# The output projection of a fused attention and MLP kernel: from two slots a tile with partial sums in DRAM to four slots a tile without them

## The chip, the cores and the metric

One core of one Trainium2 chip runs the whole program. The metric is device time in microseconds (us) of one execution. The kernel before took 1678.53 us, the median of three runs (1677.63 to 1680.38).

## The reference, cut to what matters

```python
# x: [1, 2048, 512] f32; wqkv: [512, 1536]; wo: [512, 512]; w1: [512, 1792]; w2: [1792, 512]; H = 32, Dh = 16
xn = layernorm(x)
q, k, v = split(xn @ wqkv)                       # 32 heads of 16
s = softmax(q @ k.T * Dh**-0.5) @ v @ wo          # the last product is "WO" below
h = xn @ w1 + b1
r = where(h > 0, h, 0)
g = silu((r * r) @ w2 + b2)
out = x + s * g
```

## The kernel before, in words

**Units, slots, engines.** Attention is cut into 32 units (`NU`): a unit is four heads (a quad, eight of them) by 512 queries (a chunk, four of them), unit u being quad u // 4 and chunk u % 4. A unit has 16 slots, one for each 128 keys, so the main loop has 512 slots. In slot `st` TensorE makes four score products (`exp_mm`, tile `se`, line 1222), ScalarE takes their exponential (`pt`, line 1228), and the four value products of slot `st - 2` follow (`pv_step`, `pv_mm`, line 376; each is recorded as two matmuls, so eight records of line 376 are one slot). TensorE's order is written out by hand: it is the order in which the Python code emits.

**Maxima.** The exponential is shifted by a row maximum, from a second set of score products (`max_mm`, line 301, tile `pm_t`), 64 for each unit and 2048 in all, each reduced by VectorE (line 309). Unit u's maxima are due eight slots before its first slot (`SHIFT`). A few are made before the loop, and the rest in the slots, usually four in each. When a unit's maxima are complete, `shift` transposes them (line 337) two slots later and sends them by way of DRAM into the rows of `qe` that the scores read.

**Row tiles.** Scores and maxima contract over 64 rows: TensorE is split into two row tiles of 64 rows ("lanes"), and two such matmuls run side by side, one in each lane. Dense products (the MLP, and WO) contract over 128 rows and are cut into a lower and an upper half: one half runs in its lane while scores and maxima run in the other. Two lanes may not write one bank at once, so the halves of a product take turns. All f32 dense products are made from high and low parts: three matmuls for one product.

**Two ways to put dense work into slots.** `slot` (used for what `halves` yields) puts one half's products into one slot, opposite the scores and maxima of the other lane. `long_slots` (used for what `block` yields) takes 12 products of each half and lays them over four slots, a half over two slots. It knows two forms: where `ahead_m` says that the maxima are far enough ahead, a half gets seven maxima and the value products of its two slots stand together; else it gets eight maxima and the value products stand apart. The text calls them the form with seven and the form with eight.

**Order of the dense work.** The generator `dense` gives the loop its dense work: the MLP up to slot 451 (`mlp_tasks`, mostly `long_slots`), two slots with none, and then WO. Normalised attention rows come back from DRAM (`on_d`) as `oc`. `wo_part` makes, for 16 tiles of 128 tokens, the products with the first 384 rows of `wo` (quads 0 to 5; the last 128 rows belong to quads 6 and 7, which end late), two slots a tile by `halves`; for chunks 2 and 3 it adds quad 6's rows (`q6`, line 761). ScalarE copies the bank (line 751), GpSimd multiplies with the gate `g` and adds `x` (lines 752 and 753), and for chunks 0 and 1 the result goes to DRAM (`sp_d`). `wo_last` then adds the last 128 rows of `wo` for chunks 0 and 1, in 2 x 8 slots of three products a half; its result is multiplied by VectorE (line 781), added by GpSimd to the partial sum that is read back from `sp_d`, and stored. The last quad of chunks 2 and 3 is done by `unit_inner` and `unit_final` from the unit's own tile: three matmuls of 128 rows a tile (`unit_out`, line 828). `unit_final` is the chain behind the last value product: copy `po`, four sums (line 792), reciprocal, spreading (line 808), normalising, split into high and low, four `unit_out`, four stores.

**Banks.** PSUM has `pe` (3 banks, tile `se`), `pm` (3, tile `pm_t`), `pd` (1, tile `pd_t`, the dense products) and `pv` (1, tile `po`). After the last maximum `slot` and `plain_slot` lend every second score a `pm` bank. Before the loop, the last of the projection is drained by

```python
while far:
    step([lambda: max_mm(0)] + [None] * 4)
```

where `step` issues one entry of its list and one of `far` in turns.

Of the kernel before, what the change touches and what calls it, by code (L numbers as in the profile page):

```python
# [16 lines left out]
P = 128  # L17
# [23 lines left out]
def kernel(  # L41
# [21 lines left out]
    sp_d = dram.tile([S, D], F32, name="sp_d")  # L63
# [33 lines left out]
    with ExitStack() as ph:  # L97
# [558 lines left out]
        def wo_pools():  # L656
            wos["f"] = right(wstk, "fp", 4)
            wos["oc1"] = right(wstk, "oc1p", 1)
            tp = tail["p"] = right(wstk, "tailp", 1)
            wos["oc3"] = right(o3, "oc3p", 2)  # L660

        def wo_small():

            tp = tail["p"]
            raw = wos["f"].tile([P, D], F32, name="s")
# [12 lines left out]
        def wo_load(c, kos):  # L678
            if len(kos) > 1:
                oc = wos["oc3"].tile([P, 2, len(kos), 512], F32R, name="oc")  # L680
            else:
                oc = right(wstk, f"oc1{c}p", 1).tile([P, 2, 1, 512], F32R, name="oc") if c else wos["oc1"].tile([P, 2, 1, 512], F32R, name="oc")

            for a, b in ((0, P), (P, 512)) if len(kos) > 1 and c == 0 else ((0, 512),):
                for n, ko in enumerate(kos):
                    nc.sync.dma_start(
                        oc[:, :, n, a:b].bitcast(F32),
                        on_d[ko][:, :, c * 512 + a : c * 512 + b].rearrange("k p t -> p k t"),
                    )
            wos["t" if len(kos) > 1 else "l", c] = oc  # L690

        def wo_terms(ps, oc, tt, kos):
            wot = wos["w"]
            ts_ = slice(tt * P, (tt + 1) * P)
            return terms3(ps, [
                (lambda a, q, n=n: oc[q, a, n, ts_], lambda b, q, ko=ko: wot[q, b, ko])
                for n, ko in enumerate(kos)
            ])

        def wo_ask(k):  # L700

            c, tt = divmod(k % 16, 4)
# [3 lines left out]
            if k < 16:  # L706
                t = wos["oc3"].tile([P, D], F32, name="xr", bufs=3)
                nc.sync.dma_start(t, xf[t0 : t0 + P, :])
            elif c < 2:
                t = wos["f"].tile([P, D], F32, name="s")  # L710
                nc.sync.dma_start(t, sp_d[t0 : t0 + P, :])
            else:
                t = tail[c, tt]
            wos[k] = g, t

        def wo_part():
            q6s = []
            for c in range(4):
                for tt in range(4):
                    k = 4 * c + tt  # L720
                    if c < 3 and tt == (1 if c == 0 else 0):
                        wo_load(c + 1, [0, 1, 2])
                    if k in (4, 8):

                        q = wos["oc3"].tile([64, 2, 512], F32R, name="q6", bufs=2)
                        nc.sync.dma_start(
                            q.bitcast(F32),
                            on_d[3][:, :64, (k // 4 + 1) * 512 : (k // 4 + 2) * 512].rearrange(
                                "k p t -> p k t"
                            ),  # L730
                        )
                        q6s.append(q)
                    if k in (8, 12):
                        q6 = q6s.pop(0)
                    if k < 14:
                        wo_ask(k + 2)
                    if k == 14:
                        wo_load(0, [3])
                        wo_ask(16)
                        wo_ask(17)  # L740
                    ps = pd.tile([P, D], F32, name="pd_t")
                    t0 = c * 512 + tt * P
                    ts_ = slice(tt * P, (tt + 1) * P)
                    g, xr = wos.pop(k)
                    if c > 1:
                        s = tail[c, tt] = tail["p"].tile([P, D], F32, name=f"ts{c}{tt}")
                    else:
                        s = wos["f"].tile([P, D], F32, name="s")

                    def post():  # L750
                        nc.scalar.activation(s, ps, AF.Copy)
                        nc.gpsimd.tensor_tensor(s, s, g, op=ALU.mult)  # L752
                        nc.gpsimd.tensor_tensor(s, s, xr, op=ALU.add)  # L753
                        if c < 2:
                            later(2, lambda s=s, t0=t0: nc.sync.dma_start(sp_d[t0 : t0 + P, :], s))

                    it = halves(wo_terms(ps, wos["t", c], tt, [0, 1, 2]), (9,), post, 1)
                    own, end = next(it)
                    if c > 1:
                        own = own + [  # L760
                            lambda a=a, b=b: nc.tensor.matmul(
                                ps, q6[:, a, ts_], wos["w"][:64, b, 3],
                                start=False, stop=False, skip_group_check=True,
                            )
                            for a, b in ((0, 0), (0, 1), (1, 0))
                        ]
                    yield own, end
                    yield from it

        def wo_last(c):  # L770
            for tt in range(4):
                k = 16 + 4 * c + tt
                wo_ask(k + 2)
                if k == 19:
                    wo_load(1, [3])
                t0 = c * 512 + tt * P
                g, s = wos.pop(k)
                ps = pd.tile([P, D], F32, name="pd_t")

                def post():  # L780
                    nc.vector.tensor_tensor(g, ps, g, op=ALU.mult)
                    nc.gpsimd.tensor_tensor(g, g, s, op=ALU.add)
                    later(1, lambda g=g, t0=t0: nc.sync.dma_start(of[t0 : t0 + P, :], g))

                yield from halves(wo_terms(ps, wos["l", c], tt, [3]), (3,), post, 1)


# [36 lines left out]
        def unit_out(ps, c, tt, add):  # L824
            hl, w7 = tail["hl"], tail["w7"]
            ts_ = slice(tt * P, (tt + 1) * P)
            for n, (i, k) in enumerate(((0, 0), (0, 1), (1, 0))):
                nc.tensor.matmul(  # L828
                    ps, hl[:, i, ts_], w7[:, k], start=(n == 0), stop=(n == 2)
                )  # L830
            k = 16 + 4 * c + tt
            g, s = wos.pop(k)
            t0 = c * 512 + tt * P
            if k < 28:
                wo_ask(k + 2)
            if k == 27:
                later(2, lambda: [wo_ask(30), wo_ask(31)])
# [7 lines left out]
        def unit_inner(po):  # L845
# [7 lines left out]
            def out(tt):  # L853
                tail["hl"] = ev["hl"]
                unit_out(pm.tile([P, 512], F32, name="pm_t"), 2, tt, nc.gpsimd)
# [4 lines left out]
        def unit_final(po):  # L860
            ot = tail["ot"] = tail["p"].tile([P, 512], F32, name="tot")
            nc.scalar.activation(ot[:, :256], po[:, :256], AF.Copy)
# [3 lines left out]
            for tt in range(4):  # L866
                unit_out(
                    pm.tile([P, 512], F32, name="pm_t"), 3, tt, nc.vector if tt % 2 else nc.gpsimd
# [338 lines left out]
        while far:  # L1207
            step([lambda: max_mm(0)] + [None] * 4)
# [4 lines left out]

        def exp_mm(st, j, pts, spare):
# [3 lines left out]
            if spare:  # L1218
# [27 lines left out]
        def dense():  # L1246
# [4 lines left out]
            wo_load(0, [0, 1, 2])  # L1251
            wo_ask(0)
            wo_ask(1)
            for _ in range(2):
# [3 lines left out]
            for c in range(2):  # L1258
                if c == 0:
                    o3.close()  # L1260
                else:
                    for _ in range(4):
                        yield None, None
                yield from wo_last(c)
# [47 lines left out]
        def long_slots(st0, units, post):  # L1312
# [26 lines left out]
            for h in range(2):  # L1339
# [3 lines left out]
                if ahead_m(sum(done_m) + 7, st + 2):  # L1343
                    visit(h, "s" + "D" * 12 + "s", ".mmsmssmsmssmm")
# [5 lines left out]
                else:  # L1350
                    visit(h, "D" * 10, "msmsmsmsms")
# [4 lines left out]
                    visit(h, "DDss", "mmsm", True)  # L1356
# [36 lines left out]
        for st_ in range(NU * 16):  # L1393
# [11 lines left out]
            if item is not None and len(item) > 2:  # L1405
                assert st_ % 4 == 0
                long_slots(st_, *item[:2])
# [39 lines left out]
```

## Time and profile before

| what | value |
|---|---|
| median of three runs | 1678.53 us |
| profiled execution: its own time | 1678.24 us |
| profiled execution: span from first to last instruction | 1676.4 us |
| TensorE busy (matmuls) | 1638.3 us, 98% |
| TensorE weight loads | 989.4 us, 59% |
| VectorE, ScalarE, GpSimd busy | 80%, 71%, 32% |
| mean granted TensorE clock | 0.998 |

Matmuls are pipelined and their ends are modelled, so a TensorE that is busy 98% of the span isn't one that works at its fastest. In the views, PE is TensorE, PEld its weight loads, DVE VectorE, ACT ScalarE, POOL GpSimd, SPq the queue that issues DMAs. L203, L235, L301 and so on are line numbers of the kernel before.

### The profile page before, as it was taken

The numbers are of one execution on the slowest core, as the hardware profiler recorded it, in microseconds if no ns is written. First come the engines' busy times: TensorE is split into PE (matmuls) and PEld (weight loads), VectorE is DVE, ScalarE is ACT, GpSimd is POOL, SyncE is SP. The second block draws the span as 40 slices with busy tenths as digits, with TensorE's granted clock in tenths as the row PEclk, the third lists the DMA queues.
The fourth block names the chain that finished last, engine by engine and source line by source line (L and its number), as shares of the span: only waits on it lengthen the run. The fifth ranks groups of instructions, "written<-read, shape, count | busy, mean of one in ns | idle before, by whom it ended". The sixth has DMA issues, their size and how long they took to land.

```text
span 1676.4 us, 36115 instructions
## 1 busy us (share of the span) xinstructions
PE 1638.3 (98%) x13692; PEld 989.4 (59%) x13692; DVE 1336.7 (80%) x2294; ACT 1191.5 (71%) x2354; POOL 529.7 (32%) x548
## 2 busy tenths in 40 slices
PE   6999999999999999999999999999999999999998
PEld 5898665556656655665565456545654565555533
DVE  6499888887888778778788888888888888888512
ACT  7221577778878877887777777777777777766685
POOL 4435566523212221231132123212320233143333
PEclk9999999999999999999999999999999999999999
DMA  8577555426233532353243324352335332167344
GB/s 283 167 236 254 192 162 151 130 78 162 61 90 103 141 84 68 117 129 89 55 145 93 87 79 127 79 127 80 113 80 105 99 110 68 33 206 208 102 139 134
DMA packets 156726, 208.05 MB, mean 124 GB/s; under 512 B 51272, under 2 KB 71240, under 8 KB 155016
## 3 DMA queue, kind: packets, MB, share of 16 engines
q1 hardware_dynamic: 156552, 205.74, 43.5%
q8 instruction: 108, 1.77, 0.4%
q14 instruction: 66, 0.54, 0.1%
HBM read 149.30 MB, written 56.09 MB: 123 GB/s over the span
## 4 chain that ended last, share of the span: by engine, by line
PE 85%; issue 5%; POOL 3%; DMA 3%; DVE 2%; ACT 1%; SPq 0%; POOLq 0%; ACTq 0%; DVEq 0%
PE po L376 26%; PE pd_t L235 16%; PE pm_t L301 15%; PE se L1222 14%; PE pd_t L203 5%; PE se L987 3%; PE se L938 2%; PE pd_t L987 1%; DVE mx L309 1%; PE po L987 1%; POOL ts L753 1%; POOL ts L752 1%; PE pm_t L828 1%; DMA sm<-ot 0%; POOL s L753 0%
## 5 line engine op out<-in xcount | busy, mean ns | idle before, releaser
L309 DVE TENSOR_REDUCE mx<-pm_t 128x1 f32<-128x512 f32 x2048 | 1265.3, 682 | 232.6 <-PE pm_t L301 128.2
L1228 ACT ACTIVATE pt<-se 128x512 f32<-128x512 f32 x1720 | 912.8, 613 | 253.3 <-PE se L1222 182.8
L301 PE MATMUL pm_t<-ka,qm 64*128 64x512 f32 x2048 | 780.7, 415 | 4.5 <-DVE mx L309 3.9
L1222 PE MATMUL se<-qe,ka 64*128 64x512 f32 x1988 | 739.1, 415 | 0.0
L376 PE MATMUL po<-pt,v 128*32 128x512 f32 x3560 | 527.7, 603 | 0.0
L301 PEld LDWEIGHTS pm_t<-ka,qm 64*128 64x128 f32 x2048 | 359.8, 184 | 194.2 <-DVE mx L309 181.3
L1222 PEld LDWEIGHTS se<-qe,ka 64*128 64x128 f32 x1988 | 348.9, 184 | 103.0 <-ACT pt L1228 59.8
L235 PEld LDWEIGHTS pd_t<-xc,w1s 64*128 64x128 f32 x2352 | 295.4, 187 | 46.5 <-issue 44.4
L235 PE MATMUL pd_t<-xc,w1s 64*128 64x256 f32 x2352 | 321.3, 286 | 0.0
L235 PE MATMUL pd_t<-w2t,hT 64*128 64x512 f32 x936 | 252.6, 406 | 0.0
L376 PE MATMUL po<-ex,v 128*32 128x512 f32 x536 | 208.3, 602 | 0.0
L1228 ACT ACTIVATE ex<-se 128x512 f32<-128x512 f32 x268 | 160.0, 615 | 39.9 <-PE se L1222 22.2
L235 PEld LDWEIGHTS pd_t<-w2t,hT 64*128 64x128 f32 x936 | 160.3, 184 | 43.4 <-issue 35.2
L376 PEld LDWEIGHTS po<-pt,v 128*32 128x32 f32 x3560 | 88.0, 108 | 152.8 <-issue 135.7
L550 POOL TENSOR_TENSOR r<-r 128x512 f32<-128x512 f32 x49 | 51.0, 1041 | 317.9 <-ACT r L547 317.9
L569 POOL TENSOR_TENSOR u<-u,b_t 128x512 f32<-128x512 f32 x16 | 20.6, 1287 | 283.5 <-ACT u L568 253.9
L203 PE MATMUL pd_t<-w2t,hT 64*128 64x512 f32 x408 | 106.4, 392 | 2.0 <-POOL w2t L81 1.2
L414 POOL TENSOR_TENSOR ot<-ot,hl 128x512 f32<-128x512 f32 x31 | 39.8, 1285 | 216.9 <-DMA hl<-r_d 166.7
L203 PE MATMUL pd_t<-wot,oc 64*128 64x512 f32 x336 | 90.9, 406 | 9.0 <-DVE mx L309 6.1
L203 PEld LDWEIGHTS pd_t<-wot,oc 64*128 64x128 f32 x336 | 58.4, 184 | 58.1 <-ACT pt L1228 16.3
L203 PEld LDWEIGHTS pd_t<-w2t,hT 64*128 64x128 f32 x408 | 72.7, 184 | 11.4 <-POOL w2t L81 1.6
L82 POOL TENSOR_TENSOR hT<-r,hT 128x512 fp32r<-128x512 f32 x56 | 72.3, 1291 | 4.7
(124 smaller groups left out, 1245.2 us busy)
## 6 DMA issues: line engine op xcount, KB each, us to landing
w1s<-w_d SPq DMA_DIRECT2D x196, 256.0 KB
qm<-q_d SPq DMA_DIRECT2D x384, 32.0 KB
qe<-q_d SPq DMA_DIRECT2D x384, 32.0 KB
ka<-k_d SPq DMA_DIRECT2D x96, 128.0 KB
xn_d<-xT SPq DMA_DIRECT2D x8, 1024.0 KB
k_d<-hl SPq DMA_DIRECT2D x32, 256.0 KB
q_d<-hl SPq DMA_DIRECT2D x32, 256.0 KB
xc<-xn_d SPq DMA_DIRECT2D x16, 512.0 KB
```

The lines of the kernel that those rows point to most:

```text
L82: (lo or nc.gpsimd).tensor_tensor(dst[1], raw, dst[0].bitcast(F32), op=ALU.subtract)
L203: mm = nc.tensor.matmul(out_, lh(r), rh(r), start=first_ and lane == 0, stop=last_ and lane == 1, skip_group_check=True,)
L235: mm = nc.tensor.matmul(out_, lh(r), rh(r), start=first_ and lane == 0, stop=last_ and lane == 1, skip_group_check=True,)
L301: nc.tensor.matmul(ps, qms[u][p][64 * j : 64 * j + 64, qb * P : (qb + 1) * P], kas[qd, p][64 * j : 64 * j + 64, kc * 512 : (kc + 1) * 512] ...
L309: return nc.vector.tensor_reduce(mxs[u][:, c, kc : kc + 1], ps, axis=AX.X, op=ALU.max)
L376: nc.tensor.matmul(po[32 * j : 32 * j + 32, :], vs[qd][:, (4 * kb + j) * VW : (4 * kb + j) * VW + 32], pts[j], start=(kb == 0), stop=(kb = ...
L414: nc.gpsimd.tensor_tensor(ot, ot, hl[:, 1].bitcast(F32), op=ALU.mult)
L550: nc.gpsimd.tensor_tensor(r, r, r, op=ALU.mult)
L938: nc.tensor.matmul(out_, lh(slice(0, P)), rh(slice(0, P)), start=first_, stop=last_)
L987: inst = nc.tensor.matmul(out_, lh(r), rh(r), start=first_ and lane == 0, stop=last_ and lane == 1, skip_group_check=True,)
L1222: nc.tensor.matmul(se, kas[qd, j // 2][b : b + 64, kb * P : (kb + 1) * P], qes[u][j // 2][b : b + 64, :], start=True, stop=True,)
L1228: return nc.scalar.activation(pts[j], se, AF.Exp, scale=0.25)
```

## The change

- **WO moves into `long_slots`**: 14 tiles of 128 tokens in 14 groups of four slots, the last 56 slots of the loop (456 to 511; the MLP still ends at 451, and slots 452 to 455 have no dense work). The order (`WO_ORDER`) is chunk 2 (four tiles), the first two tiles of chunk 3, chunk 0, chunk 1. Each tile has its full sum at once: 12 products a half for chunks 0 and 1, and 12 and 9 for chunks 2 and 3, whose last quad still comes from the unit's tile.
- **No partial sums in DRAM**: `sp_d`, `wo_last` and the `q6` loads go; `oc` holds all four 128-row parts of a chunk in one of three buffers, the last part loaded by `wo_load_last` when its units are done.
- **Both halves at once**: a group of chunk 0 or 1 that begins when all maxima are made and no shift is pending (`m_free`) is "wide": three `pm` banks are kept, one for the upper half's sum, two for scores. Both lanes then run dense products and scores side by side in ten steps for two slots, and VectorE multiplies the two banks, with two additions on GpSimd.
- **The last two tiles** (chunk 3, tiles 2 and 3) get their 24 products as matmuls of 128 rows outside the loop: 13 ahead of the last two value steps, 2 while the unit's tile is copied, 4 behind the sums, 5 behind the normalising products. `unit_out` then adds to these banks, and takes these two tiles first.
- **Smaller**: `ahead_m` no longer counts extra maxima in WO slots; the drain ahead of the loop makes one maximum with each three entries of `far` where it was five; unit 30's `unit_out` uses an `se` bank instead of a `pm_t` bank; four more `pt` buffers.

```diff
-        def wo_load(c, kos):
...
+        def wo_load(c):
+            oc = wos["oc"].tile([P, 2, KO, 512], F32R, name="oc")
+            if c == 3:
+                nc.gpsimd.memset(oc[64:, :, 3].bitcast(F32), 0.0)
...
+        def m_free():
+            return not (todo_m[0] or todo_m[1] or late)
+
         def wo_part():
...
+            for k in range(14):
+                c, tt = WO_ORDER[k]
+                if k == 0:
+                    later(8, lambda: wo_load(3))
+                    later(12, lambda: wo_load_last(3))
+                if k == 4:
+                    wo_load(0)
+                if k == 6:
+                    later(1, lambda: wo_load(1))
+                if k == 5:
+                    wo_load_last(0)
+                if k == 9:
+                    wo_load_last(1)
...
+                wide = c < 2 and m_free()
+                if wide and "w" not in free_ps:
+                    free_ps["w"] = [pm.tile([P, 512], F32, name="pm_t") for _ in range(3)]
+                ps = [pd.tile([P, D], F32, name="pd_t")]
+                ps.append(free_ps["w"][2] if wide else ps[0])
...
+                def post():
                     if c > 1:
+                        nc.scalar.activation(s, ps[0], AF.Copy)
                         nc.gpsimd.tensor_tensor(s, s, g, op=ALU.mult)
                         nc.gpsimd.tensor_tensor(s, s, xr, op=ALU.add)
+                        return
+                    if wide:
+                        h = wos["f"].tile([P, D], F32, name="h", bufs=2)
+                        nc.vector.tensor_tensor(h, ps[1], g, op=ALU.mult)
+                        nc.gpsimd.tensor_tensor(xr, xr, h, op=ALU.add)
+                    nc.vector.tensor_tensor(g, ps[0], g, op=ALU.mult)
+                    nc.gpsimd.tensor_tensor(g, g, xr, op=ALU.add)
+                    later(2, lambda g=g, t0=t0: nc.sync.dma_start(of[t0 : t0 + P, :], g))
...
+                yield (units, post, 4) + ((True,) if wide else ())
...
-        def wo_last(c):
...
+        def fill_mms():
+            oc, wot = wos["oc", 3], wos["w"]
+            for tt in (2, 3):
+                ps = tail["ps", tt] = free_ps["w"][tt - 2]
...
+                    fill.append(lambda ps=ps, a=a, b=b, n=n, ts_=ts_, m=m: nc.tensor.matmul(
+                        ps, oc[:, a, n, ts_], wot[:, b, n], start=m == 0, stop=False,
+                        skip_group_check=True,
+                    ))
...
         def unit_final(po):
...
+            run_fill(2)
             unit_sums(pe, "se")
+            run_fill(4)
             unit_norm(pe, "se", (nc.vector, nc.gpsimd))
-            for tt in range(4):
+            run_fill(len(fill))
+            tail["ps", 0] = free_ps["w"][2]
+            tail["ps", 1] = pd.tile([P, 512], F32, name="pd_t")
+            for n, tt in enumerate((2, 3, 0, 1)):
                 unit_out(
-                    pm.tile([P, 512], F32, name="pm_t"), 3, tt, nc.vector if tt % 2 else nc.gpsimd
+                    tail["ps", tt], 3, tt, nc.vector if n % 2 else nc.gpsimd, tt > 1
                 )
...
         while far:
-            step([lambda: max_mm(0)] + [None] * 4)
+            step([lambda: max_mm(0)] + [None] * 2)
...
+            if "w" in free_ps:
+                spare = s_bank[0] % 5 in (1, 3)
...
         def ahead_m(n, st):
-            wo0 = 16 * NU - 62
-            for u in range(n // 64, NU):
-                end = 16 * u - SHIFT
-                n_max = n + 4 * max(0, end - st)
-                n_max += max(0, min(end, wo0 + 32) - max(st, wo0))
-                if n_max < 64 * (u + 1):
-                    return False
-            return True
+            return all(
+                n + 4 * max(0, 16 * u - SHIFT - st) >= 64 * (u + 1) for u in range(n // 64, NU)
+            )
...
+                n = len(units[h])
+                if wide:
+                    for i, o in enumerate("sDDsDDsDsD"):
+                        for lane in range(2):
+                            if o == "s":
+                                s(lane)
+                            else:
+                                units[lane].pop(0)()
+                    if wrap and not units[0]:
+                        wrap.pop()()
+                    begin(st + 1)
+                    for kb in (st - 2, st - 1):
+                        pv_step(kb, pts.pop(kb))
+                elif ahead_m(sum(done_m) + 7, st + 2):
+                    visit(h, "s" + "D" * n + "s", ".mmsmssmsmssmm")
...
+        run_waiting(True)
         assert not waiting and next(dn, None) is None
+        fill_mms()
+        run_fill(13)
         for st_ in (NU * 16 - 2, NU * 16 - 1):
             pv_step(st_, pts.pop(st_))
```

More of the change, by code (lines that the diff above doesn't have):

```diff
@@ L705, in wo_ask @@
             nc.sync.dma_start(g, g_d[t0 : t0 + P, :])
-            if k < 16:
-                t = wos["oc3"].tile([P, D], F32, name="xr", bufs=3)
+            if (c, tt) in tail:
+                t = tail[c, tt]
+            else:
+                t = wos["f"].tile([P, D], F32, name="xr", bufs=4)
                 nc.sync.dma_start(t, xf[t0 : t0 + P, :])
[L709 to L713, printed above, removed]
@@ L752, in post @@
                         nc.gpsimd.tensor_tensor(s, s, g, op=ALU.mult)
                         nc.gpsimd.tensor_tensor(s, s, xr, op=ALU.add)
[L754 to L766, printed above, removed]
@@ L767, in wo_part @@
-                    yield own, end
-                    yield from it
-        def wo_last(c):
[L771 to L785, printed above, removed]
+                        return
@@ new lines, in post, with emit @@
+                    if wide:
[5 more added lines that the diff above has]
+                    later(2, lambda g=g, t0=t0: nc.sync.dma_start(of[t0 : t0 + P, :], g))
+                def emit(lane, n, i, m, kos):
+                    r = slice(64 * lane, 64 * lane + 64)
+                    a, b = ((0, 0), (0, 1), (1, 0))[i]
+                    inst = nc.tensor.matmul(
+                        ps[lane], oc[r, a, n, ts_], wot[r, b, n],
+                        start=m == 0 and (lane == 0 or wide), stop=m == kos and (lane == 1 or wide),
+                        skip_group_check=True,
+                    )
+                    if m == 0 and last_use[0] is not None and not wide:
+                        tc.add_manual_dep(
+                            inst.ins, last_use[0].ins.name,
+                            mybir.DependencyInfo(
+                                mybir.DependencyClass.Sync, mybir.DependencyReason.DATA
+                            ),
+                            reason="the other row tile is done with the bank",
+                        )
@@ L789, in unit_sums, with run_fill @@
+        def run_fill(n):
+            for _ in range(min(n, len(fill))):
+                fill.pop(0)()
         def unit_sums(pool, name):
@@ L854, in out @@
                 tail["hl"] = ev["hl"]
-                unit_out(pm.tile([P, 512], F32, name="pm_t"), 2, tt, nc.gpsimd)
+                unit_out(pe.tile([P, 512], F32, name="se"), 2, tt, nc.gpsimd)
             for tt in range(4):
@@ L1250, in dense @@
             wo_pools()
-            wo_load(0, [0, 1, 2])
+            wo_load(2)
+            later(1, lambda: wo_load_last(2))
             wo_ask(0)
             wo_ask(1)
-            for _ in range(2):
+            for _ in range(4):
                 yield [], None
@@ L1257, in dense @@
             yield from wo_part()
[L1258 to L1264, printed above, removed]
         pts = {}
@@ L1406 @@
                 assert st_ % 4 == 0
-                long_slots(st_, *item[:2])
+                long_slots(st_, item[0], item[1], len(item) > 3)
                 done = st_ + 4
```

135 lines of the change are left out of this document (69 added, 66 removed).

## The prediction, made before the changed kernel ran

> **What bounds the kernel now.** I read the page first, then the stages in the view of windows restricted to line 376 (eight records are one slot, so the count gives the slots), then the waits of the last stage, then the timeline of the end.
>
> ```profile
> span 1676.4 us, 36115 instructions
> PE 1638.3 (98%) x13692; PEld 989.4 (59%) x13692; DVE 1336.7 (80%) x2294; ACT 1191.5 (71%) x2354; POOL 529.7 (32%) x548
> L203 PE MATMUL pd_t<-wot,oc 64*128 64x512 f32 x336 | 90.9, 406 | 9.0 <-DVE mx L309 6.1
> ```
>
> TensorE holds the time, but its 98% doesn't say how well: the same slot costs very different times by stage. Columns of the next fence: stretch, length, PE busy (records of line 376), PEld busy, granted clock, DMA share, GB/s.
>
> ```profile
> 372.17:471.47 99.30, 34.63 (x288) 7.51 (x288) 1.00 0.41 111
> 1297.36:1423.28 125.92, 46.88 (x352) 6.92 (x352) 1.00 0.36 94
> 1471.76:1477.16 5.40, 2.13 (x16) 0.32 (x16) 1.00 0.63 163
> 1477.16:1528.71 51.55, 14.92 (x112) 2.20 (x112) 1.00 0.71 221
> 1528.71:1537.18 8.47, 2.13 (x16) 0.31 (x16) 1.00 0.71 204
> 1537.18:1599.66 62.48, 17.04 (x128) 2.52 (x128) 1.00 0.47 129
> 1599.66:1617.98 18.32, 8.52 (x64) 1.26 (x64) 1.00 0.58 167
> 1617.98:1625.54 7.56, 4.26 (x32) 0.63 (x32) 1.00 0.39 135
> 1625.54:1643.54 18.00, 8.52 (x64) 1.26 (x64) 1.00 0.41 133
> 1643.54:1654.33 10.79, 4.26 (x32) 0.63 (x32) 1.00 0.47 133
> 1654.33:1658.28 3.95, 2.13 (x16) 0.32 (x16) 1.00 0.51 143
> ```
>
> Row by row: `long_slots` with seven maxima a half takes 99.30 us for 36 slots, 11.03 us a group of four; with eight maxima 125.92 us for 44 slots, 11.45 us a group, shifts and evacuations included; slots without dense work 2.70 us. Then WO: the 32 slots of `wo_part` take 51.55 + 8.47 + 62.48 = 122.50 us, 3.68 us a slot with nine products and 3.9 us in the later ones; the 16 slots of `wo_last` 18.32 + 18.00 us; four slots of scores alone 7.56 us; four slots with unit 30's `unit_out` 10.79 us; the last two 3.95 us. From the end of slot 453 to the value products of the last but two slots: 181.12 us for 58 slots. This stretch is what the change rewrites. Why a WO slot costs so much shows in the waits from 1477 to 1658 us (total, times, longest):
>
> ```profile
> PEld pd_t L203 <- ACT pt L1228: 16.3, 17, 1.2
> PEld pd_t L203 <- DVE mx L309: 15.1, 13, 1.2
> PEld pd_t L203 <- ACT s L751: 9.7, 8, 1.3
> PEld pd_t L203 <- ACT ts L751: 7.8, 7, 1.3
> ```
>
> WO's weight loads stand 49 us, for scores and maxima that the same slot issued too fast for ScalarE and VectorE, and once a tile for the copy that frees the one `pd` bank. No DMA is in these lines.
>
> The pitch of TensorE's work comes from the timeline:
>
> ```profile
> 1640.78 0.39 PE L1222 MATMUL se<-qe,ka 64*128 64x512 f32 x1
> 1641.01 0.39 PE L1222 MATMUL pm_t<-qe,ka 64*128 64x512 f32 x1
> 1621.21 0.18 PEld L1222 LDWEIGHTS pm_t<-qe,ka 64*128 64x128 f32 x1 [0.27 <-ACT pt L1228]
> 1647.68 0.96 PE L828 MATMUL pm_t<-w,hl 128*128 128x512 f32 x3
> 179.30 6.81 DVE L309 TENSOR_REDUCE mx<-pm_t 128x1 f32<-128x512 f32 x11 [0.33 <-PE pm_t L301]
> ```
>
> In a lane one step is 0.23 us (1640.78 to 1641.01). Three 128-row matmuls take 0.96 us, of which the last one is 0.50 in the modelled end, so they follow each other at 0.23 us too. Reduces follow at 6.81 / 11 = 0.62 us.
>
> **The change, part by part.**
>
> *Work.* Before, WO is 336 + 24 = 360 half products. After: 8 tiles of 24 and 6 of 21, 318 halves, and 24 full matmuls worth 48 halves. So TensorE's work doesn't shrink (366 for 360); all that can be won is how it is packed.
>
> *Maxima.* The maxima left at 1477.16 us, by the weight loads of line 301 in the three WO stretches:
>
> ```profile
> 1477.16:1528.71 51.55, 29.11 (x71) 12.85 (x70) 1.00 0.71 221
> 1528.71:1537.18 8.47, 4.32 (x11) 1.83 (x10) 1.00 0.71 204
> 1537.18:1599.66 62.48, 23.66 (x57) 10.28 (x56) 1.00 0.47 129
> ```
>
> 70 + 10 + 56 = 136 at slot 454. Before the end, `ahead_m` compares n - 4 st with 96 for every unit, in the old and the new form, so the lead of 136 is the same after the change. Slots 454 and 455 make eight of them, and 128 are left at slot 456: eight groups with 16 each, up to slot 487. Unit 31's shift is then pending for two slots, so the group at 488 isn't wide, and has no maxima; the five groups from 492 on are wide.
>
> *Groups of WO with maxima: eight.* They are the form with eight maxima, 11.45 us each, 91.6 us: same 24 products of 512 columns or fewer, same scores. Reduces need 16 x 0.62 = 9.9 us of it. Six end with a ScalarE copy, as MLP groups do. Two (chunk 0) end with VectorE's product, which queues behind up to three reduces and then keeps `pd` from the next group; I bound this by 0 and 1.3 us (the longest wait for a copy above) and take 0.5 each, 1.0.
>
> *The group at 488*: the form with seven, 11.03 us; without maxima hardly less, since a half's 14 steps stay.
>
> *Five wide groups.* Ten steps for a half where the form with seven has 14: 11.03 - 8 x 0.23 = 9.2 us is the lower bound. ScalarE needs 7.56 us (the four slots of scores alone, 16 exponentials, are held by it: 0.47 us each), so it isn't the bound over a group. But eight scores of a half come within eight steps (1.9 us) and have five banks; the sixth to eighth wait for the first to third exponential, as in the row at 1621.21 (0.27). I take 0.2 us a half, 9.6 us a group, 48.0 us. Upper bound 11.03: no gain over the old form. The sums' banks are free in time: VectorE has nothing else, and two products of 0.69 us (the rows of line 838 below) lie under 2.2 us of value products.
>
> *Unit 30's `unit_out`*: 10.79 - 7.56 = 3.2 us as today; the `se` bank is read within a slot.
>
> The sum from slot 454 to 511: 5.40 + 91.6 + 1.0 + 11.0 + 48.0 + 3.2 = 160.2 us for 181.1: **-20.9**.
>
> *Fill.* 13 full matmuls stand ahead of the last two value steps. Their exponentials are ready by then (ScalarE ends a half before TensorE does), so nothing hides the fill: 13 x 0.23 and a change of tiling, **+3.2** (0 if ScalarE lags, 5.9 at half clock). In return the last two value steps no longer wait for exponentials: **-0.3**.
>
> *The last chain.* Columns of the first two rows: PE, PEld, DVE, ACT, POOL busy, clock, DMA.
>
> ```profile
> 1661.40:1665.70 4.30, 2.22 (x16) 1.95 (x16) 1.86 (x5) 0.72 (x3) 0.00 (x0) 0.93 0.30 104
> 1665.80:1670.70 4.90, 4.88 (x12) 3.81 (x12) 2.58 (x5) 0.30 (x1) 2.02 (x2) 0.50 0.05 19
> ...
> 1661.83 1.06 PE L792 MATMUL se<-sel,tot 128*128 128x4 f32 x8 [0.47 <-ACT tot L862]
> 1663.70 1.16 PE L808 MATMUL se<-ident,rs 128*128 128x128 f32 x8 [0.81 <-DVE rs L799]
> 1665.82 5.49 PE L828 MATMUL pm_t<-w,thl 128*128 128x512 f32 x12 [0.96 <-ACT thl L818]
> 1666.18 0.73 POOL L820 TENSOR_TENSOR thl<-tot,thl 128x256 fp32r<-128x256 f32 x1 [10.29 <-ACT thl L818]
> 1667.57 0.69 DVE L838 TENSOR_TENSOR g<-pm_t,g 128x512 f32<-128x512 f32 x1 [1.34 <-PE pm_t L828]
> 1672.13 0.97 DVE L839 TENSOR_TENSOR g<-g,ts 128x512 f32<-128x512 f32 x1
> ```
>
> The clock falls to 0.50 just as the 12 `unit_out` matmuls begin, after 4 us in which TensorE was half idle: they take 0.43 us each, and VectorE gets its first bank at 1667.57. The fills of 2, 4 and 5 need 0.5, 0.9 and 1.2 us and meet stops of 0.47, 0.81 and 0.96 us: some 0.2 us late. They keep TensorE busy, and I take the clock as full. The new order needs columns 256 to 511 first, whose low part POOL has at 1666.91, so the first bank comes no sooner; from there VectorE alone sets the end: four products and two additions of 0.7 to 0.9 us back to back, 4.4 us, where 1667.57 to 1673.10 are 5.5: **-1.1**. The Trainium skill's page "TensorE: Matmul & The Clock Gate", in Part 1 on the clock gate, has the clock halved after an idle window of about 3.4 us and restored after a busy one. By that rule TensorE, never idle that long here, would not have slowed at all, and the fill would win nothing; the trace disagrees, with 0.50 after stops of at most 1 us. So half idle is enough to lose it, and how much filling keeps it isn't shown: that is a rival.
>
> *Ahead of the loop.* 23 entries are drained in eight steps for five, so three more maxima, in a stretch where VectorE reduces without a gap (the row at 179.30): 3 x 0.62, **+1.8** (0 if a later gap takes it). The three maxima let three more halves keep the form with seven: 3 x (11.45 - 11.03) / 2 = **-0.6**.
>
> *DMA and queues.* The stores and loads of `sp_d` go. `oc` is asked for four slots (11 us) ahead at the first group, where it was two and no wait shows. SP waits with the last part of `oc` for the stores of quad 7; behind it stand `q` loads for a unit 16 slots away and shift rows due in six. I cost this at nothing; its cover is the 11 us, and a chunk that comes later than that makes TensorE wait for the rest.
>
> **Sum**: 1.8 - 0.6 - 20.9 + 3.2 - 0.3 - 1.1 = -17.9 us. The profiled execution took 1678.24 (span 1676.4 and 1.8 around it): 1660.3, and 0.3 more against the median of 1678.53: **1660.5 us**.
>
> **Rivals.**
>
> *WO groups keep the rate of WO slots (slower).* If it is WO's own products behind the waits of line 203, and not the way `slot` lays them, the eight groups cost four slots of 3.68, 14.7 us: +26 less the 1.0 already counted, 1685.5. It decides from 13.7 us a group (11.45 + 17.9 / 8). For: the 49 us of waits name line 203. Against: the releasers are scores, maxima and the copy, all of which MLP groups have at 11.45 us. Chance 0.06.
>
> *The wide groups are held by scores and their banks*: 11.03 us each, +7.0: 1667.5. For: row 1621.21, where six banks already wait. Against: 2.2 us of value products in which ScalarE catches up. Chance 0.13.
>
> *The clock falls in the last chain all the same*: -1.1 goes, and fills of 0.43 us are up to 1 us late: 1662.5. Chance 0.07.
>
> *A full TensorE*: work is equal, TensorE is 98% busy, so nothing is won, the fill and the drain are added: 1678.5 + 3.2 + 1.8 - 2.0 = 1681.5. Against: the 3.68 us of a nine-step slot, where nine steps and the value products are 2.1 + 1.1. The page "Perfetto Trace Analysis" of the Trainium skill, section "Identifying the Most-Contended Engine", calls matmul busy time no good measure, because matmuls are pipelined, and asks for the weight loads' share; here that is 59%, and the rows agree. Chance 0.04.
>
> **How the numbers follow.** Forecast 0.70. Less than 0.2% (3.4 us) is about what a measurement here can't tell from none. Faster: 0.70 + 0.13 + 0.07 = 0.90. The full TensorE lies 3.0 us above, mostly within the bound: same 0.03, and 0.01 of it with the slower rival, slower 0.07. Range: unknowns down (wide 9.2, no VectorE waits, drain hidden, fill half hidden) reach 1655; up, the rival of wide groups and 1 to 2 us of fill at half clock reach 1669; the two slow cases (0.10) and the tails stay out.
>
> **What would show it.** Groups between slots 456 and 487 at 11.3 to 11.6 us (slower rival: over 13.7); five wide groups at 9.2 to 10, with 11 as the rival; the waits of line 203 for `s`, `mx` and `pt` gone; about 3 us between the value products of slots 509 and 510; the clock in the last 10 us at 1.00; three maxima more ahead of the loop. The forecast is wrong if any stage is outside these by more than 3 us, above all if TensorE waits for `oc`.

## The result, and the profile after

The changed kernel takes 1665.88 us, the median of four runs (1663.79 to 1667.31), against 1678.08 us of four runs of the kernel before. The ratio is 0.9926, with a 95% interval of 0.9909 to 0.9943: 12.2 us less, where 17.9 were forecast. One execution of the experiment `drain_recip` took 8059 us and one of the kernel before 8154 us, and both are left out of what follows. The profiled execution took 1665.91 us, its span is 1664.1 us.

```profile
span 1664.1 us, 35934 instructions
PE 1633.2 (98%) x13674; PEld 981.0 (59%) x13674; DVE 1341.3 (81%) x2299; ACT 1185.3 (71%) x2344; POOL 511.2 (31%) x534
```

By shares of busy time nothing happened. The stages tell it. The next fence is the windows view of the changed kernel, restricted to the value products (now line 375; columns: stretch, length, PE busy, PEld busy, clock, DMA share, GB/s; eight records a slot).

```profile
1479.61:1485.02 5.41, 2.13 (x16) 0.32 (x16) 1.00 0.95 309
1485.02:1519.38 34.36, 12.78 (x96) 1.89 (x96) 1.00 0.47 141
1519.38:1534.87 15.49, 5.13 (x32) 0.67 (x32) 0.89 0.44 117
1534.87:1580.94 46.07, 17.05 (x128) 2.53 (x128) 1.00 0.50 157
1580.94:1592.19 11.25, 3.86 (x32) 0.86 (x36) 1.00 0.23 50
1592.19:1620.23 28.04, 11.55 (x100) 2.51 (x96) 1.00 0.35 111
1620.23:1643.50 23.27, 7.70 (x68) 1.67 (x64) 1.00 0.57 183
1643.50:1647.68 4.18, 1.04 (x12) 0.13 (x4) 1.00 0.19 70
```

Row by row: two slots without dense work; three WO groups at 11.45 us; one group of 15.49 us with the clock at 0.89; four groups at 11.52; the group that isn't wide; three wide groups at 9.35 us; two wide groups that hold unit 30's `unit_out`, 11.6 us each; and 4.18 us from the value products of slot 509 to those of slot 510. The same 58 slots that took 181.12 us take 163.89. What went are the 49 us for which WO's weight loads stood:

```profile
PEld pm_t L300 <- DVE mx L308: 19.3, 33, 2.8
PEld pd_t L766 <- issue: 9.2, 10, 1.7
PEld pd_t L766 <- DVE g L759: 0.4, 2, 0.2
```

The view is of the waits from 1485 to 1660 us. WO's products (now line 766) wait for no score, no maximum and no ScalarE copy any more; the longest of the waits that are left, 19.3 us, stands at the maxima (line 300), and the copy's shows at the scores, with 5.0 us. These are waits of weight loads. TensorE was without a matmul for 10.0 us of the 181.1 before and for 3.8 us of the 163.9 after, so most of what was won was counted as busy time.

Set against the forecast's terms, from the two profiled spans (1676.4 and 1664.1, 12.3 less):

| term | forecast | measured |
|---|---|---|
| ahead of slot 454 (drain, forms, shifts) | +1.2 | +2.4 |
| eight WO groups with maxima | 92.6 | 95.9 |
| the group at slot 488 | 11.0 | 11.25 |
| five wide groups and `unit_out` | 48.0 + 3.2 | 46.7 + 4.6 |
| 13 fills | +3.2 | +3.3 |
| last two value steps and last chain | -1.4 | -0.9 |

So the gain is there, and it is 5.6 us smaller than forecast: 1.2 are lost ahead of the rewritten stretch, 3.3 in the groups with maxima (the fourth is 4.0 us over the others, which are a little better than forecast), 0.5 in the last chain, and some tenths elsewhere. The time alone, 1665.9, lies nearer to the rival of wide groups held by scores (1667.5) than to the forecast (1660.5); only the stages tell the two apart. The experiments look at the places, and at what made the gain.

### The profile page after: what moved, and what is told of

Read it like the earlier page. It is cut to its first block, busy times and chain, and to the rows that moved or that the text cites. A ratio compares the mean times of both kernels' runs of the same rounds, so it can differ in the third digit from the quotient of the medians.

```text
span 1664.1 us, 35934 instructions
## 1 busy us (share of the span) xinstructions
PE 1633.2 (98%) x13674; PEld 981.0 (59%) x13674; DVE 1341.3 (81%) x2299; ACT 1185.3 (71%) x2344; POOL 511.2 (31%) x534
## 4 chain that ended last, share of the span: by engine, by line
PE 93%; DVE 3%; DMA 2%; issue 1%; ACT 1%; POOL 0%; SPq 0%; DVEq 0%; POOLq 0%; ACTq 0%
PE po L375 29%; PE pd_t L234 16%; PE pm_t L300 16%; PE se L1255 15%; PE pd_t L202 6%; PE se L1013 3%; PE pd_t L766 2%; DVE mx L308 2%; PE se L964 2%; PE pd_t L1013 1%; PE po L1013 1%; DMA xc<-xn_d 1%; DMA sm<-ot 1%; PE pm_t L336 1%; DMA xt<-in_A_x_dram 0%
## 5 line engine op out<-in xcount | busy, mean ns | idle before, releaser
L1261 ACT ACTIVATE pt<-se 128x512 f32<-128x512 f32 x1750 | 926.7, 615 | 234.7 <-PE se L1255 150.2
L1255 PEld LDWEIGHTS se<-qe,ka 64*128 64x128 f32 x2016 | 353.2, 184 | 113.9 <-ACT pt L1261 68.4
L375 PE MATMUL po<-ex,v 128*32 128x512 f32 x532 | 213.3, 602 | 0.0
L766 PE MATMUL pd_t<-wot,oc 64*128 64x512 f32 x258 | 75.8, 410 | 0.0
L1013 PE MATMUL se<-xT,wr_t 64*128 64x512 f32 x312 | 66.2, 391 | 0.0
```

What stands on the lines that cost most here:

```text
L375: nc.tensor.matmul(po[32 * j : 32 * j + 32, :], vs[qd][:, (4 * kb + j) * VW : (4 * kb + j) * VW + 32], pts[j], start=(kb == 0), stop=(kb = ...
L766: inst = nc.tensor.matmul(ps[lane], oc[r, a, n, ts_], wot[r, b, n], start=m == 0 and (lane == 0 or wide), stop=m == kos and (lane == 1 or ...
L1013: inst = nc.tensor.matmul(out_, lh(r), rh(r), start=first_ and lane == 0, stop=last_ and lane == 1, skip_group_check=True,)
L1255: nc.tensor.matmul(se, kas[qd, j // 2][b : b + 64, kb * P : (kb + 1) * P], qes[u][j // 2][b : b + 64, :], start=True, stop=True,)
L1261: return nc.scalar.activation(pts[j], se, AF.Exp, scale=0.25)
```

## The experiments

All comparisons are with the kernel before, run on the same chip. Single executions of one program differ by 2 to 7 us, much of it in the first 36 slots (107 to 113 us in the profiles), so where an edit is worth little the stage is compared and not the time. A stage is from one profile of each kernel.

**The changed kernel again.**

> The changed kernel once more, as the measure for the other runs on this chip: 1665.9 us within 2. In its first profile TensorE stood 2.8 us in slot 468 with VectorE's reciprocal of unit 28 ahead of the maxima, and the stall shows again if it belongs to the program (theory), and is gone or elsewhere if it was a chance of that execution (rival).

1668.23 us; ratio 0.994 (0.9926 to 0.9953). The group from the value products of slot 465 to those of 469 takes 15.59 us again, the other seven with maxima 11.3 to 11.7: the stall belongs to the program.

**Where the 3.3 us of the fourth group went.** The waits from 1519 to 1531 us of the changed kernel, and rows of its timeline:

```profile
PEld pm_t L300 <- DVE mx L308: 4.7, 4, 2.8
DVE sm L399 <- DMA sm<-ot: 2.9, 1, 2.9
...
1517.67 3.82 SPq L132 DMA_DIRECT2D qm<-q_d  x6
1521.59 0.62 SPq L393 DMA_DIRECT2D sm<-ot  x1
1523.56 0.25 DVE L399 RECIPROCAL sm<-sm 128x16 f32<-128x16 f32 x1 [2.85 <-DMA sm<-ot]
1524.41 0.61 PE L300 MATMUL pm_t<-ka,qm 64*128 64x512 f32 x1 [2.36 <-DVE mx L308]
```

SP spends 3.82 us on six issues of `q` loads, so the DMA with unit 28's sums is issued at 1521.59 and lands two microseconds later. VectorE has come to the reciprocal by then and waits 2.85 us with the maxima's reductions queued behind it. No `pm` bank comes free, TensorE stands, and in the windows view the granted clock of the 3.6 us from 1524.40 is 0.53. The edit gives the reciprocal of units 28 and 29, its store and its read-back one slot more:

```diff
-            steps = EVAC_LAST if u >= 28 else EVAC
+            steps = (1, 4, 5, 6, 7, 9) if u >= 28 else EVAC
```

> Only units 28 and 29 have their reciprocal, its store and its read-back one slot later (steps 1, 4, 5, 6, 7, 9 for 1, 3, 4, 5, 7, 9). Theory: in slot 468 VectorE's reciprocal waits for the sums' DMA, which SP issued late behind q loads; the maxima behind it wait, TensorE stands and its clock halves. One slot later the DMA is there: slots 468 and 469 fall from 9.85 us to 5.7, the time by about 4 us to 1662. Rival: TensorE stood for oc's or the maxima's own loads: no change within 0.5 us.

1663.85 us; 0.9915 (0.9903 to 0.9928). The group, in the same view of this kernel:

```profile
1520.11:1531.41 11.30, 4.26 (x32) 0.63 (x32) 1.00 0.38 107
```

11.30 us for 15.5, and 4.4 us less than the changed kernel's 1668.23 on the same chip: shown.

**The drain ahead of the loop.** Only this line is put back:

```diff
-            step([lambda: max_mm(0)] + [None] * 2)
+            step([lambda: max_mm(0)] + [None] * 4)
```

> Only the drain ahead of the loop is put back to one maximum with five entries. Theory: the three extra maxima cost about 2.4 us ahead of slot 454 (the loop starts 3.4 us later, and every shift from slot 260 on stands in an odd slot behind scores and maxima, 0.3 us more each, against 1.3 us won by three halves in the form with seven). So the value products of slot 451 come back from 1479.6 to 1477.2 within 0.5, and the time falls by 2.4 us, by up to 6.5 if the moved maxima also take the stall of slot 468 away. Rival: the 2.4 us come with the new tiles and loads, and the drain is worth nothing or its old price of 1.2: slot 451 stays at 1478.5 to 1479.6.

1667.7 us; 0.9934 (0.9921 to 0.9946), 0.5 us below the changed kernel beside it, which is inside the intervals. Slot 451's value products do come back to 1477.15 us. But the end gives it back: the maxima finish later, the group of slots 492 to 495 isn't wide and takes 11.06 us for 9.35, and the eight groups with maxima take 97.8 us for 95.9 and 96.1, the stall of the fourth group among them (16.2 us). The forecast of this run saw the first half only. The new drain, seen by itself as a loss, pays for a fifth wide group.

> Both edits together. Theory: they are separate places, 2.4 + 4.2 us, about 1659.3. If the old drain alone moves the maxima's loads away from the sums' DMA, the two overlap and the time is no better than that of the better one by more than 1 us. Rival (neither is the cause): 1665.9 within 1.5.

With the later reciprocal too: 1662.75 us; 0.9905 (0.989 to 0.992), where 1659.3 was expected. That is 1.1 us below the later reciprocal alone, inside the interval: no sum of the two edits shows, as the old drain alone won nothing that shows.

**What laid the groups' gain.** The groups that aren't wide give the same products to two single slots, and two empty slots follow:

```diff
-                yield (units, post, 4) + ((True,) if wide else ())
+                if wide:
+                    yield units, post, 4, True
+                else:
+                    yield units[0], None
+                    yield units[1], post
+                    yield [], None
+                    yield [], None
```

> The groups that aren't wide give their 12 and 12 or 12 and 9 products to two single slots, as the kernel before laid its WO work, and two slots without dense work follow; the same products in the same 56 slots. Theory: it is the laying over four slots that wins, so the six groups of slots 456 to 479 go from 11.3 us to 13 to 14 each (4.4 + 3.6 + 2 x 2.7), 10 to 15 us in all. Rival (full sums and no partial sums in DRAM are what wins): under 0.5 us a group.

1678.76 us; 1.0012 (1.0001 to 1.0022). Stages of this kernel, three and two groups without the fourth's stall:

```profile
1486.20:1525.83 39.63, 12.79 (x96) 1.89 (x96) 1.00 0.42 124
1543.93:1569.96 26.03, 8.53 (x64) 1.26 (x64) 1.00 0.45 134
```

13.2 and 13.0 us a group for 11.45, with the same sums and no partial sums in DRAM. The waits are back too: in these groups WO's weight loads stand 8.5 us for maxima and 6.7 us for exponentials (none for the copy, which the two empty slots cover). In the time the whole gain is gone, though the maxima finish earlier and a sixth group is wide. The 58 slots take 175.6 us, 11.7 more than in the changed kernel, and its fourth group, with the stall, 18.1. So laying a tile over four slots is what wins most. Against the 181.1 us before, 5.5 us are still won in this stretch. By the next experiment its six wide groups are worth some 8 us, and the stall costs 5, so I estimate that about 2 us are left for the full sums; no run has them alone.

**Wide groups.** `wide` is always False; the fill takes its banks after the loop.

> No group is wide: the five groups from slot 492 on are in the form with seven, without maxima, both halves in one bank, scores in three banks. Theory: a group costs 11.2 us as the one at slot 488 does, for 9.34 when wide, so 9.5 us more: 1675.4. Rival: the wide groups win only what ScalarE and the banks allow, and without them ScalarE catches up: under 3 us more.

1675.43 us; 0.9986 (0.9975 to 0.9998).

```profile
1598.71:1631.27 32.56, 11.54 (x100) 2.50 (x96) 1.00 0.37 114
1631.27:1656.78 25.51, 7.69 (x68) 1.67 (x64) 1.00 0.44 146
```

The first row is three groups at 10.85 us for 9.35, the second two groups with `unit_out`, 25.51 us for 23.27: 58.07 us for 51.31 in all. So being wide is worth 1.5 us in a group, 1.1 in one with `unit_out`, and 6.8 us in all; less than the 9.5 expected from the group at slot 488, whose 11.25 us hold a shift; more than the rival allowed. That the median came out at the expected 1675.4 is luck: the changed kernel wasn't run on this chip, and the stage is 2.7 us off.

**The fill and the clock.** First without the 24 matmuls, so that the last two tiles lack these products:

> The 24 fill matmuls are left out (the last two tiles lack their products with quads 0 to 6). Theory: the 13 ahead of the last value steps cost 3.2 us, and the rest keep TensorE's clock at full in the last chain; without them the value products of slot 510 follow those of 509 in 0.9 us for 4.2, the clock is 0.5 when the unit_out matmuls run at 0.43 us each, and the chain from the last value product to the end is 0.5 to 1.5 us longer: 2 to 3 us less in all. Rival (the clock doesn't hang on the fill): the clock stays at 1.00 and the whole 3.3 us and a bit are won.

1664.98 us; 0.9924 (0.9907 to 0.994). The windows view (PE, PEld, DVE, ACT, POOL busy, clock, DMA share, GB/s) of this kernel's last chain, then of the changed kernel's:

```profile
1645.60:1650.30 4.70, 2.23 (x16) 1.95 (x16) 2.13 (x6) 1.10 (x3) 0.00 (x0) 0.96 0.15 56
1650.30:1653.50 3.20, 3.11 (x8) 2.38 (x9) 0.85 (x2) 0.04 (x1) 1.39 (x2) 0.53 0.00 0
```

```profile
1649.60:1654.40 4.80, 4.71 (x29) 3.57 (x27) 2.17 (x6) 1.14 (x3) 0.00 (x0) 1.00 0.00 0
1654.40:1657.80 3.40, 3.28 (x12) 2.10 (x12) 1.68 (x4) 0.00 (x0) 1.97 (x2) 1.00 0.01 2
```

Without fill TensorE is busy 2.23 of 4.70 us, and `unit_out` runs at 0.53; with it 4.71 of 4.80, and the clock stays at 1.00. The fill holds the clock: shown. It costs 3.3 us ahead of slot 510 and gives back 0.9 behind it (17.3 us from there to the end without fill, 16.4 with it). The time doesn't show these 2.4 us: the ratio is that of the changed kernel, which wasn't run on this chip.

Then with the 13 taken from ahead of the last value steps and put behind tiles 0 and 1, on top of the later reciprocal:

```diff
-        run_fill(13)
...
-            run_fill(len(fill))
+            run_fill(5)
...
-            for n, tt in enumerate((2, 3, 0, 1)):
+            for n, tt in enumerate(range(4)):
+                run_fill((0, 0, 1, 12)[tt])
```

> On top of the later reciprocal: no fill ahead of the last value steps; 2, 4 and 5 as before, tiles 0 and 1 of the last chunk first, then one more fill, tile 2, twelve fills, tile 3. Theory: the 13 are 3.3 us that nothing hides, and behind tiles 0 and 1 they run under VectorE's products; slot 510 follows 509 in 0.9 us, the last chain grows by about 1 us, 2.3 us less in all than 1663.85. Rival: without the 13 the clock falls as it does without any fill, the twelve take 0.43 us each, 5 us, and the chain grows by 3 us or more: nothing won.

1660.81 us; 0.9908 (0.9895 to 0.9921), and once more:

> The kernel with the later reciprocal and the fills behind once more, as the measure on the same chip: 1660.8 within 1.5; the sum of both edits against the changed kernel is 4.2 + 2.7 us, so a ratio to the kernel before of 0.988 to 0.991.

1660.94 us; 0.9897 (0.9881 to 0.9914). Slot 510 and the last chain of this kernel:

```profile
1640.15:1641.01 0.86, 0.86 (x12) 0.26 (x8) 1.00 0.44 162
```

```profile
1643.00:1647.50 4.50, 4.50 (x27) 3.48 (x28) 1.88 (x6) 0.85 (x3) 0.00 (x0) 1.00 0.16 58
1647.50:1653.00 5.50, 5.50 (x25) 4.47 (x25) 3.23 (x5) 0.28 (x1) 3.17 (x3) 1.00 0.26 97
```

0.86 us for 4.18; the eleven fills in the stops are enough for the clock in the first of these rows, and with the rest behind tiles 0 and 1 it holds in the second; the stretch from slot 510 to the end grows from 16.4 to 17.0 us. 2.7 us are won in the profile. Against the later reciprocal alone the ratios say 1 to 3 us, with intervals of 2 us either way.

**The shifts.** Timeline of the kernel before, then of the changed one, at one unit's transpose (`m` against `ident`):

```profile
1359.89 0.40 PE L235 MATMUL pd_t<-xc,w1s 64*128 64x256 f32 x2
1360.22 0.28 PE L337 MATMUL pm_t<-ident,m 128*16 128x128 f32 x1
```

```profile
1352.85 0.39 PE L1255 MATMUL se<-qe,ka 64*128 64x512 f32 x1
1353.36 0.09 PEld L336 LDWEIGHTS pm_t<-ident,m 128*16 128x16 f32 x1 [0.55 <-DVE mx L308]
1353.36 0.28 PE L336 MATMUL pm_t<-ident,m 128*16 128x128 f32 x1
```

With three more maxima made ahead of the loop a unit's maxima are complete in another half of a group, and the transpose follows scores and the last reduction by 0.51 us, where it followed dense products by 0.21 (the second of the two matmuls in the row at 1359.89 starts at 1360.01). On top of the later reciprocal:

```diff
-                    late.append((now[0] + 2, u))
+                    late.append((now[0] + 2 + (now[0] % 2 if 18 <= u < 31 else 0), u))
```

> On top of the later reciprocal: for units 18 to 30 the shift falls due in the next even slot. Theory: since the three extra maxima, units complete half a group later, and the transpose stands in an odd slot, straight behind scores and the maximum's last reduction, where TensorE waits 0.5 us for 0.2; in an even slot it follows dense products. Some 12 shifts at 0.2 to 0.3 us: 2.4 to 3.6 us less than with the later reciprocal alone (1663.85), of which about 2 between the value products of slots 268 and 451. Rival: the extra time between slots 268 and 428 is the maxima's own, wherever the transpose stands: within 0.7 us of 1663.85.

1663.5 us; 0.9926 (0.9914 to 0.9938): no better. The transposes do stand 0.2 to 0.33 us behind again, and the stretch from slot 268 to slot 451 takes 525.0 us for 526.4, 1.4 us and not 2 (524.4 to 525.3 in the three kernels with even shifts, 526.4 to 527.3 in the eight others with the new drain). But the fourth group has its stall back:

```profile
1517.83:1530.79 12.96, 4.26 (x32) 0.63 (x32) 1.00 0.42 114
```

```profile
1519.91 2.80 SPq L132 DMA_DIRECT2D qm<-q_d  x6
1522.80 0.61 SPq L393 DMA_DIRECT2D sm<-ot  x1
1524.78 0.25 DVE L399 RECIPROCAL sm<-sm 128x16 f32<-128x16 f32 x1 [2.33 <-DMA sm<-ot]
```

The sums' DMA leaves SP still later, and one slot no longer covers it. That is why a third edit was expected to add up and didn't:

> Later reciprocal, even shifts and the fills behind. Theory: separate places that add up, about 5 us less than 1663.85, 1659. If the fills behind lose the clock, only the 2.4 to 3.6 us of the shifts: 1661.

1662.11 us; 0.9909 (0.9896 to 0.9922), with 12.69 us in the fourth group. With a second slot for the reciprocal, `(1, 5, 6, 7, 8, 9)`:

> Even shifts and fills behind, and unit 28's and 29's reciprocal two slots later than in the changed kernel (steps 1, 5, 6, 7, 8, 9). Theory: with even shifts SP issues the sums' DMA 1.2 us later still, behind twelve q loads, so that one slot was not enough: the group of slots 467 to 470 kept a 1.4 us stall with VectorE's reciprocal ahead of the maxima. With two slots the stall goes (11.3 us for 12.7), and the time falls by 1.4 us against the even shifts with one slot, to 1660.7. Rival: SP's queue is the limit, the stall moves to the next group or to the store of unit 28's rows, and nothing is won.

1659.4 us; 0.9889 (0.9874 to 0.9903), the shortest median of all, 1.5 us below `fill_behind_2` on the same chip, whose interval overlaps with it. The fourth group and slot 510:

```profile
1519.74:1531.05 11.31, 4.26 (x32) 0.63 (x32) 1.00 0.33 91
1639.57:1640.42 0.85, 0.85 (x12) 0.26 (x8) 1.00 0.51 193
```

## Why the prediction was right or wrong, point by point

The direction, the mechanism and most terms were right; the gain was forecast 5.6 us too large. (1660.3 and 0.3 make 1660.6, not 1660.5.)

- **WO groups**: right. 11.45 us forecast; 11.45 and 11.52 measured outside the fourth group; behind one of the two chunk-0 groups 0.4 us are lost, where 1.0 was put down. The slower rival (13.7 us and more) is out. `slots_for_groups` lays these products the way the kernel before did and comes near it, with 13.0 to 13.2 us and the waits back: they come from how `slot` lays the work, not from WO's products.
- **The fourth group**: the step that failed is "I cost this at nothing" under *DMA and queues*. By the sign that the prediction set itself, no stage outside by more than 3 us, this group fails: 15.49 us is 3.9 over 11.6. I looked for TensorE waiting for `oc`. What waited was VectorE's reciprocal, for a small DMA that SP issued behind `q` loads, each of some 0.6 us of issue; the maxima were the queue behind the waiting instruction. It cost 4.2 us, by the later reciprocal. The kernel before had such a wait too, of 1.6 us, in a slot that took 4.8 us where those beside it took 3.7, so I estimate that it lost about 1 us by it.
- **Ahead of slot 454**: the term was mis-sized. The drain is as forecast, 1.8 us: the first value products come at 196.4 us in the mean of the profiles with the new drain (195.4 to 197.1), at 194.6 in three with the old one (193.8 to 195.3). The halves in the form with seven won more than the 0.6 put down: slots 232 to 268 fell from 104.1 to 101.4 us (103.2 and 103.6 with the old drain, so about 2 us are the drain's). What I left out is that the slots in which units are complete move by half a group, which puts the shifts in odd slots: 1.4 us from slot 268 on, by `even_shift`; slots 36 to 232 grew by 1.3 us too, and fall back with `old_drain` (546.6, 548.0 and 546.8 us), but no run tried the shifts alone there.
- **Wide groups**: 9.35 us, below the 9.6 of the forecast and near its lower bound of 9.2: so by my own sum the five banks held the scores up by under 0.1 us a half, where I took 0.2. The rival of 11.03 is refuted. That only five of six groups are wide came as worked out.
- **Unit 30's `unit_out`**: 4.6 us for 3.2, a mis-sized term. I took the price from slots that ScalarE held (7.56 us for four), where a part of the three matmuls may have run in TensorE's idle time. In the wide groups three matmuls take 0.96 us, 3.8 for four tiles, and beside them stand waits of 0.2 to 0.4 us for `hl` and for a bank; in `no_wide` the four cost 3.8 us in all (25.51 for two groups of 10.85). No run takes this term apart, so its cause is argued.
- **Fill**: +3.3 us, as forecast, not hidden.
- **Last chain**: the clock stayed at 1.00, so that rival is out; `no_fill` shows that the fill does it. The last two value steps are 0.3 us shorter, as forecast (1.92 us for 2.19 from slot 510's first record to the last end). The chain behind them won 0.6 us and not 1.1, a mis-sized term: from its first product VectorE needs 5.1 us, where I added up 4.4 without a stop. It waits 0.42 us for the second bank, and its last addition takes 1.25 us, beside a GpSimd addition, for the 0.97 before.

```profile
1656.90 0.69 DVE L859 TENSOR_TENSOR g<-pm_t,g 128x512 f32<-128x512 f32 x1 [0.42 <-PE pm_t L848]
1659.09 1.26 POOL L860 TENSOR_TENSOR g<-g,ts 128x512 f32<-128x512 f32 x1 [1.23 <-DVE g L859]
1659.64 1.25 DVE L860 TENSOR_TENSOR g<-g,ts 128x512 f32<-128x512 f32 x1
```

- **A full TensorE**: refuted. It is 98% busy before and after. The 58 slots fell from 181 to 164 us with 318 half products of WO for 360, but with the 24 matmuls outside the loop the work is 366 for 360, and from slot 454 to the end of the kernel it takes 184.5 us for 199.2.

## What to carry to other kernels

Judge a busy engine by the time that one unit of its work takes in each stage: a stage whose slot costs more than its steps is where the order can win, even at 98% busy and with the work unchanged. When a stage is made faster, go through every engine's queue for small waits that the slow version hid: here a reciprocal of 0.25 us, held by a DMA behind other issues, stopped three engines. And a fill that keeps the clock is free only where the engine stands anyway: put it into the stops, not ahead of the chain.

## What the runs showed of the hardware that was not expected

The granted clock falls without a stop of 3 us. In the traces it stands at 0.50 for 3.41 us, for twice that, or until the program ends, and as far as they show, it hangs on how long matmuls were busy in the 3.41 us ahead of the drop: 1.05 us in the fourth group, with a stop of 2.4 us; 1.76 us in `no_fill`, with no stop longer than 1.3 us; 2.22 us in the last chain of the kernel before, with none longer than 1 us. In `fill_behind` 2.27 us of 3.42 kept it at 1.00. Taken over all 14 profiles, in steps of 3.41 us, each of 29 drops followed at most 2.22 us of matmuls, and no step with more lost the clock; between 1.98 and 2.22 both are found (estimates, since the ends of matmuls are modelled). The Trainium skill's page "TensorE: Matmul & The Clock Gate", Part 1, asks for an idle window of about 3.4 us. The length agrees, but by these rows a window that is busy for more than half of it can count as idle.

And issue time on SP is a resource: six loads of 32 KB took 2.7 to 4.5 us to issue, and the small DMA behind them in the fourth group left only when they were through.
